# Duo attention and PReLU MLP on one core: the first 400 steps in another order

## Chip, cores, metric

The kernel runs on 1 core of one Trainium2 chip. The metric is the device time of one execution in microseconds (us), lower is better. The core has a matrix engine (PE, with its weight loads shown as PEld), three engines for elementwise work (DVE, ACT, POOL) and SP, which here only issues DMAs. Each takes its own instructions strictly in the order in which the program lists them, and waits at semaphores for the others.

## Reference

Attention for 4 batches of 8 heads, 768 tokens, head size 64, and then a two-layer MLP on the 3072 tokens.

```python
scores = scale * np.matmul(q, k.transpose(0, 1, 3, 2))
# causal mask for heads 0, 2, 6 ("retrieval"); the other heads ("streaming") keep
# of the causal part only the 4 first keys and the last 64
scores = np.where(mask[None], scores, -1e9)
a = np.exp(scores - np.max(scores, axis=-1, keepdims=True))
a = a / (np.sum(a, axis=-1, keepdims=True) + 1e-09)
x = (a @ v).transpose(0, 2, 1, 3).reshape(3072, 512)
h = x @ w_in                                   # 512 -> 2048
g = np.maximum(h, 0.0) + alpha * np.minimum(h, 0.0)
out = g @ w_out                                # 2048 -> 512
```

Inputs and outputs are float32; the kernel computes in bfloat16 with float32 sums.

## The kernel before

The work is cut into some thousand named items. `ORDER`, a string near the top, lists the 1076 names, and the last loop of the kernel calls them one after the other. Each call appends its instructions to the queues of the engines that it uses, so ORDER sets the order on every engine, and with it the order of the DMA issues, of the PSUM banks that are taken and given back (`take`, `give`: the free bank that has been free longest), and of the rings of buffers.

The heads are treated in 16 segments n, each a pair of heads of one batch (`PAIRS`: one batch is four segments). The names:

- `Lq`, `Lk`, `Lv` n: loads of q, k and v by SP (one half of Lk0 by ACT). Segment n uses buffer n % 4 of each, so that a load waits for the casts of segment n-4.
- `Cq`, `Ck`, `Cv`: casts to bfloat16, on POOL, DVE or ACT by the strings CQ, CK, CV. `Tq`, `Tk`: transposes on PE for n < 8; `tq`, `tk`: their copies out of PSUM (DVE for the first four `tk`, ACT for `tq` and for `tk` of n from 4 on). From n = 8 on a DMA transposes.
- `S` n.hh.m: scores of head hh, part m, on PE; `s`: their exp on ACT; `m`: mask on DVE (n from 4 on; for n < 4 the mask is added by a matmul with `nms` or `nmr`). `A`: probabilities times v on PE; `a`: division on DVE; `X`, `x`: transposed into `xT` (PE and DVE for n < 4).
- `P` t.f: first MLP layer for token block t (512 or 256 tokens) and rows f, on PE; P0.f.0 to P0.f.2 are its parts for f < 6. `p`: relu of the negative on ACT; `g`: the PReLU on DVE (L609). `O` t.s.u: a quarter of the second layer; `o`: the copy on ACT and the store.
- `wi0` to `wi7`, `wo0` to `wo3`: loads of the MLP's weights, issued by POOL. They fill what P and O of those rows need.
- `warm`: matmuls of zeros on PE, as fillers (L687; 32, 3, 14 and six times 4 of them). `id`, `idf`, `zero`, `one`, `busy`, `kz`, `vz`, `qz`, `sz`, `so`, `ro`, `vo`, `nz`, `kfz`: constants and memsets. `nr` makes mr_near on POOL from `one`; `ns` makes ms_near with twelve POOL instructions. `La`, `Al`, `al`: the slopes.

Scores of n from 4 on are not issued at once. They are gathered as a burst until an item comes that may not stand beside them:

```python
if min(columns) < SPLIT:            # SPLIT = 576; columns of the two heads hh
    for x in burst:
        nc.tensor.matmul(*x[3:6], start=True, stop=True)      # L423, 128 rows
else:                               # alternately, each on its own 64 rows: L430
```

With enough columns of both heads the two halves of the array work side by side (L430); else every matmul takes the whole array (L423).

Of the kernel before, what the change touches and what calls it, by code (L numbers as in the profile page):

```python
# [19 lines left out]
X0 s2.0.1 x0 wi6 s2.0.2 wi7 Lv3 Lq5 Tq3 tk3.1 S2.0.0 wi5 m4.0.2 warm6 S2.1.0 A1.0 a1.0 Lk4 s2.0.0 A2.0 S2.1.1 A1.1  # L20
a2.0 tq3 s2.1.0 a1.1 S3.0.0 s2.1.1 s3.0.0 A2.1 a2.1 S3.1.1 X1 S3.0.1 s3.0.1 Lk5 wi4 kfz2 Cv3.0 Cq5 Lk7 wi2 X2 Ck4.0
s3.1.1 S3.1.0 x1 P0.0.0 x2 P0.0.1 A3.0 P0.1.0 P0.1.1 Lk6 Lq4 Lq6 Ck4.1 kfz3 nr Cv3.1 s3.1.0 A3.1 Lv7 Lv5 Lq7 Ck5.0 wi3
a3.0 P0.2.0 Tq5 tq5 P0.3.0 P0.3.1 a3.1 X3 x3 ns kfz1 P0.2.1 Tk4 near2 P1.2 P0.1.2 P0.2.2 P0.0.2 p1.2 p0.1 g0.1 Ck5.1
P1.0 P0.3.2 g1.2 P0.15 tk4.0 p0.2 g0.2 p0.15 wo0 p1.0 Lk8 near0 g0.15 g1.0 ro1 P1.12 P1.14 m12.1.2 p0.0 g0.0 wo1 tk4.1
p1.12 P0.14 g1.12 p0.14 g0.14 P0.13 p0.13 g0.13 P0.11 p1.14 Tk5 Ck7.1 g1.14 P1.10 tk5.0 p0.11 p1.10 Ck6.0 Ck7.0 g0.11
m8.0.2 tk5.1 wo2 Lv6 Lv4 P0.10 P0.8 p0.8 Tk7 g1.10 wo3 Cq4 Lk9 P0.12 P1.8 p0.10 g0.8 p0.12 g0.10 Tq4 P0.6 P0.9 p0.3
Ck6.1 g0.3 tq4 P0.4.0 P0.5.0 Tk6 P0.4.1 p1.8 g1.8 tk7.0 p0.9 g0.9 Cq6 P0.5.1 P0.5.2 p0.5 g0.12 p0.6 tk6.1 P0.4.2 g0.6
g0.5 tk6.0 S4.0.5 P0.7 p0.7 P1.6 g0.7 P1.4 s4.0.5 p0.4 Tq6 m4.1.2 tk7.1 g0.4 Cv5 p1.6 g1.6 O0.1.0 tq6 S4.0.3 O0.2.0
O0.2.1 S5.1.1 S5.0.0 S4.0.1 S6.1.0 m14.0.2 p1.4 g1.4 s5.0.0 O0.1.1 s4.0.3 s4.0.1 O0.2.2 S5.0.2 S5.1.0 S4.0.2 S5.1.2
s6.1.0 m4.0.1 Cv7 O0.3.0 s5.0.2 s5.1.2 s5.1.1 s4.0.2 O0.1.2 s5.1.0 O0.1.3 o0.1 Cq7 Cv4 O0.3.1 m5.1.0 m8.1.2 m5.0.2  # L30
m4.0.3 m5.1.2 S4.0.0 S4.1.4 S5.0.1 S4.0.4 S4.1.0 s4.0.4 s5.0.1 Lk10 m5.0.1 O0.2.3 O0.3.2 Tq7 m5.0.0 o0.2 s4.1.0 m4.0.4
m5.1.1 A5.1 s4.0.0 m4.0.0 a5.1 O0.3.3 tq7 S7.0.0 S7.0.1 S4.1.3 S7.1.1 S6.0.5 S4.1.1 m4.0.5 s4.1.4 o0.3 Lq9 s4.1.3 Ck8
m4.1.3 A5.0 a5.0 X5 s4.1.1 A4.0 s7.0.0 s7.1.1 Lk11 Lq8 s7.0.1 a4.0 s6.0.5 near1 m7.0.0 m7.1.1 m4.1.0 O1.1.0 S7.1.0
S6.0.4 S7.0.2 S4.1.5 S6.0.1 S7.1.2 S6.1.1 O1.1.1 Cv6 s7.1.0 O1.0.0 s4.1.5 m7.0.1 s6.1.1 m4.1.5 m6.1.1 s7.1.2 m6.1.0
s7.0.2 m7.0.2 S6.0.2 S4.1.2 S6.1.2 S6.0.0 s6.0.4 s4.1.2 s6.0.1 s6.1.2 O1.0.1 m6.0.5 m7.1.0 m4.1.1 m4.1.4 m7.1.2 m6.1.2
S6.0.3 A4.1 s6.0.0 m6.0.0 m6.0.1 A7.1 O1.1.2 A6.1 s6.0.3 m6.0.4 m6.0.3 s6.0.2 a4.1 a6.1 A6.0 A7.0 a6.0 O1.1.3 O0.0.0
O0.0.1 O0.0.2 O1.0.2 m10.0.2 O1.0.3 O0.0.3 o0.0 X4 X6 a7.1 a7.0 X7 P2.9 P2.3 p2.9 P3.4 Ck9 Cq9 g2.9 P2.14 p2.14 g2.14
Cq8 p3.4 Lq10 Lq11 Dk8.0 P2.10 p2.10 Dk9.1 o1.0 p2.3 g2.3 g3.4 Dk8.1 P3.2 P3.14 P3.12 P2.8 Dq8 P2.1 P3.8 o1.1 p3.2
Dk9.0 Lv10 g2.10 Dq9 p3.14 P2.7 Ck10 g3.2 p3.12 g3.12 g3.14 P2.2 p2.2 g2.2 Cq10 Dq10 P2.11 p2.1 g2.1 p2.11 p2.8 g2.11
P3.6 P2.5 p2.5 g2.5 P2.13 p2.13 g2.8 g2.13 P2.0 p2.0 g2.0 p2.7 P3.0 p3.0 P2.4 S8.0.5 Lv8 Lv11 P2.15 P2.12 s8.0.5 Cq11  # L40
g3.0 p2.15 g2.7 g2.15 S8.0.0 p2.12 g2.12 Ck11 p3.6 S9.0.2 P2.6 p2.6 g3.6 s8.0.0 p2.4 g2.4 g2.6 s9.0.2 p3.8 P3.10 g3.8
p3.10 O3.0.0 O2.0.0 S8.1.5 s8.1.5 O3.0.1 O2.0.1 g3.10 m8.0.0 Cv8 S8.1.3 S9.0.0 S8.0.3 S9.1.1 S8.0.1 S9.1.0 s8.1.3
s9.1.0 s8.0.1 s9.0.0 s8.0.3 m8.0.3 m8.0.1 O2.0.2 O2.0.3 o2.0 Dk10.1 Lv9 m9.0.0 Cv9 m8.0.5 Dk11.0 m9.1.0 m9.0.2 S8.0.4
S9.0.1 S10.1.1 S8.1.4 Dq11 s8.1.4 Lq13 Lk13 O3.0.2 Dk10.0 s9.1.1 s10.1.1 s9.0.1 s8.0.4 O3.0.3 o3.0 Dk11.1 S10.1.0
S10.1.2 m9.0.1 S11.0.2 S9.1.2 S8.0.2 S11.0.0 s9.1.2 Cv10 m9.1.1 A9.0 s11.0.2 s10.1.0 O2.3.0 m9.1.2 A9.1 a9.0 a9.1 X9
s10.1.2 s11.0.0 O2.3.1 Lq15 Lv14 Lq12 S8.1.0 S11.0.1 S10.0.3 m10.1.0 s8.0.2 S10.0.1 S8.1.2 S8.1.1 S10.0.0 O2.3.2
s8.1.2 s8.1.0 m8.1.4 Cq13 s11.0.1 s8.1.1 m11.0.2 m10.1.2 m8.0.4 m11.0.0 A8.0 s10.0.0 m8.1.5 m10.1.1 O2.3.3 a8.0
S11.1.2 S10.0.4 S11.1.0 S10.0.5 S10.0.2 m8.1.3 m11.0.1 s10.0.3 s10.0.1 S11.1.1 s11.1.2 A10.1 s11.1.1 O2.2.0 O2.1.0
s10.0.4 m6.0.2 m10.0.1 Cv11 m8.1.1 m8.1.0 a10.1 m10.0.4 Ck13 m10.0.0 m11.1.2 A11.0 A8.1 O2.1.1 s10.0.2 s10.0.5 o2.3
s11.1.0 Dk13.0 m11.1.1 m10.0.3 m10.0.5 m11.1.0 A10.0 a11.0 a8.1 a10.0 O3.1.0 A11.1 Cq12 O2.2.1 O2.2.2 O2.2.3 a11.1 X8  # L50
O2.1.2 O3.1.1 O3.1.2 X10 o2.2 O3.1.3 O2.1.3 X11 P4.11 o2.1 P4.14 P5.14 p5.14 P4.4 P4.6 Lk12 P5.0 g5.14 Ck12 p4.4 p4.6
p4.11 P4.13 g4.6 p4.14 g4.11 Lq14 g4.14 P5.12 P4.5 P4.12 p4.13 Dq12 o3.1 p5.0 g4.13 Cq14 g5.0 Dk13.1 p4.5 g4.5 g4.4
Cv14 P4.9 p4.9 g4.9 P4.2 P5.2 Dq13 p5.12 g5.12 P4.10 p5.2 P4.8 P4.1 p4.12 g4.12 g5.2 p4.10 g4.10 Lv15 Dk12.0 Dk12.1
Lv12 p4.1 Lk14 Lv13 Lk15 g4.1 P4.7 P4.0 p4.2 g4.2 p4.8 g4.8 p4.0 p4.7 g4.7 P4.15 Cv12 S13.0.1 s13.0.1 S12.0.5 S12.0.3
P4.3 P5.4 g4.0 s12.0.3 p4.3 s12.0.5 S12.1.5 S12.0.1 S12.0.0 S13.1.1 s13.1.1 Dq14 g4.3 Cq15 Ck14 m12.0.3 O4.3.0 s12.1.5
s12.0.1 O4.3.1 O4.3.2 s12.0.0 p4.15 g4.15 P5.6 P5.10 S12.1.1 S12.0.4 S12.0.2 p5.4 S13.1.0 g5.4 p5.6 s12.0.4 Dk14.0
P5.8 s13.1.0 s12.0.2 p5.8 s12.1.1 m12.0.0 g5.6 O4.3.3 Ck15 p5.10 g5.8 m12.0.1 g5.10 m12.0.4 O5.1.0 Cv13 O5.1.1 O5.1.2
o4.3 Dk14.1 S14.1.1 S14.0.0 S12.1.4 S14.0.1 S14.1.0 S13.0.2 m12.1.1 s14.1.0 s13.0.2 O4.2.0 m12.0.5 A12.0 s14.0.1
s12.1.4 O5.1.3 Dk15.1 s14.1.1 Dk15.0 s14.0.0 a12.0 m14.0.1 Dq15 o5.1 O4.2.1 S13.1.2 S12.1.2 S14.1.2 S14.0.4 m13.1.0
m14.0.0 m13.0.1 S14.0.5 S13.0.0 O4.2.2 O4.2.3 s13.1.2 m13.1.2 m13.1.1 s13.0.0 s14.0.4 s14.0.5 m13.0.2 S12.1.0 m12.1.5  # L60
s14.1.2 S12.1.3 S15.0.0 S14.0.3 m13.0.0 A13.1 o4.2 s12.1.0 s12.1.2 A13.0 s15.0.0 O5.0.0 s12.1.3 s14.0.3 m14.0.4 Cv15
a13.1 O5.0.1 a13.0 S15.0.1 S15.0.2 m12.1.0 S15.1.0 S15.1.2 S15.1.1 S14.0.2 O4.1.0 s15.0.2 s15.1.0 m12.1.4 s14.0.2
s15.1.1 m14.1.1 m14.0.5 m14.1.2 m12.1.3 m14.1.0 A12.1 m14.0.3 A14.1 A14.0 a14.0 s15.1.2 a14.1 m15.0.2 s15.0.1 a12.1
O4.1.1 X13 O4.0.0 O4.0.1 O4.0.2 O4.0.3 m15.0.0 m15.1.1 O4.1.2 m15.0.1 m15.1.2 m15.1.0 A15.0 o4.0 A15.1 a15.0 O4.1.3
a15.1 O5.0.2 X15 O5.0.3 X14 x15 o4.1 o5.0 X12 P6.11 p6.11 P6.2 P6.15 P6.10 p6.10 P7.4 P6.0 P6.1 g6.11 g6.10 p6.1 P6.6
P7.8 p6.15 g6.15 g6.1 p6.0 g6.0 P6.5 p7.4 p6.5 p6.6 g7.4 g6.6 g6.5 P6.3 P6.12 P7.2 p6.3 p6.12 g6.12 p6.2 g6.2 P6.4
p7.8 P7.6 P6.14 g6.3 g7.8 p7.6 p6.4 g7.6 g6.4 P7.10 P6.7 P6.8 p6.8 p6.7 P7.0 P6.9 P6.13 g6.7 p7.2 g7.2 g6.8 p7.10
g7.10 p6.9 P7.14 O6.3.0 P7.12 p6.13 g6.13 p7.12 O6.0.0 O6.0.1 O6.1.0 p7.0 g7.0 g6.9 O6.3.1 O7.0.0 O6.3.2 O6.1.1 p7.14
p6.14 g6.14 g7.12 O6.3.3 o6.3 O6.0.2 O6.1.2 O6.1.3 o6.1 O6.0.3 o6.0 O6.2.0 O6.2.1 O6.2.2 O7.0.1 O7.0.2 O6.2.3 o6.2
# [777 lines left out]
```

## Time and profile before

| | us |
|---|---|
| median of 3 runs | 229.61 (229.19 to 230.07) |
| profiled execution | 229.83 |
| its span, first to last instruction | 228.0 |
| PE busy | 222.4 |
| DVE / ACT / POOL busy | 151.6 / 139.6 / 45.8 |
| granted TensorE clock | 1.0 |

The span is what the views show; some 1.8 us of the execution lie around it. A matmul's end is modelled, and matmuls overlap, so a busy PE may still be waiting a little. In a timeline a row is a start, a length, the engine, line and operation, the tiles, how many were merged, and in brackets the idle time before and what ended it. In a row of stretches the first number is the length, then follow the busy times of PE, PEld, DVE, ACT and POOL with counts, the granted clock, the busy share of the DMA engines and GB/s.

### The profile page before, as it was taken

The numbers are of one execution on the slowest core, as the hardware profiler recorded it, in microseconds if no ns is written. First come the engines' busy times: TensorE is split into PE (matmuls) and PEld (weight loads), VectorE is DVE, ScalarE is ACT, GpSimd is POOL, SyncE is SP. The second block draws the span as 40 slices with busy tenths as digits, with TensorE's granted clock in tenths as the row PEclk, the third lists the DMA queues.
The fourth block names the chain that finished last, engine by engine and source line by source line (L and its number), as shares of the span: only waits on it lengthen the run. The fifth ranks groups of instructions, "written<-read, shape, count | busy, mean of one in ns | idle before, by whom it ended". The sixth has DMA issues, their size and how long they took to land.

```text
span 228.0 us, 5239 instructions
## 1 busy us (share of the span) xinstructions
PE 222.4 (98%) x2005; PEld 135.9 (60%) x2005; DVE 151.6 (66%) x395; ACT 139.6 (61%) x284; POOL 45.8 (20%) x91
## 2 busy tenths in 40 slices
...
DMA  6999999999998798989969899995821420000213
GB/s 190 313 229 210 286 223 262 206 197 241 206 287 142 132 204 227 172 192 181 254 153 199 194 266 146 218 166 107 132 93 38 116 95 0 0 4 0 88 66 123
DMA packets 95417, 37.39 MB, mean 164 GB/s; under 512 B 82440, under 2 KB 93600, under 8 KB 95392
## 3 DMA queue, kind: packets, MB, share of 16 engines
...
q10 hardware_dynamic: 464, 0.40, 0.5%
q8 instruction: 15, 0.25, 0.5%
...
## 4 chain that ended last, share of the span: by engine, by line
PE 92%; ACT 3%; DVE 2%; issue 1%; DVEq 0%; ACTq 0%
PE P L597 35%; PE P L617 34%; PE P L552 7%; PE P L430 4%; PE P L687 3%; PE P L413 2%; PE P L363 2%; PE P L636 2%; ACT neg L602 1%; PE P L501 1%; DVE kT L392 1%; PE P L423 1%; PE P L577 1%; ACT kT L392 1%; ACT eS L523 1%
## 5 line engine op out<-in xcount | busy, mean ns | idle before, releaser
L609 DVE SCALAR_TENSOR_TENSOR g<-neg,oma,P 128x256 bf16<-128x256 f32 (+1 forms) x128 | 71.0, 608 | 35.9 <-ACT neg L602 35.5
L597 PE MATMUL P<-xT,w_in_b 128*128 128x512 bf16 (+1 forms) x512 | 86.5, 326 | 0.0
L617 PE MATMUL P<-w_out_b,g 128*128 128x512 bf16 x368 | 85.4, 379 | 0.0
L602 ACT ACTIVATE neg<-P 128x512 f32<-128x512 f32 x96 | 54.4, 600 | 27.2 <-PE P L597 22.6
L597 PEld LDWEIGHTS <-w_in_b 128*128 128x128 bf16 x512 | 49.5, 98 | 31.7 <-DVE g L609 0.2
L617 PEld LDWEIGHTS <-g 128*128 128x128 bf16 x368 | 33.8, 98 | 37.2 <-issue 1.2
L469 ACT ACTIVATE eR<-P 128x448 bf16<-128x448 f32 (+4 forms) x63 | 37.1, 636 | 5.4 <-PE P L430 2.3
L623 ACT COPY ot<-P 128x512 f32<-128x512 f32 x23 | 13.8, 602 | 37.8 <-PE P L617 32.9
L627 POOL DMA_DIRECT2D out_dram<-ot x18 | 10.3, 571 | 113.2 <-ACT ot L623 113.0
L517 ACT ACTIVATE eS<-P 128x352 bf16<-128x352 f32 x45 | 21.0, 493 | 3.7 <-PE P L430 3.7
L563 DVE TENSOR_TENSOR xn<-P,rcp 128x448 bf16<-128x448 f32 (+1 forms) x32 | 19.5, 608 | 1.1
L528 DVE TENSOR_TENSOR eS<-eS,ms_near 128x352 bf16<-128x352 bf16 x45 | 14.3, 334 | 4.4 <-ACT eS L517 4.2
L479 DVE TENSOR_TENSOR eR<-eR,mr_near 128x128 bf16<-128x128 bf16 (+5 forms) x54 | 12.1, 252 | 4.0 <-ACT eR L469 4.0
L430 PE MATMUL P<-qT,kT 64*128 64x176 bf16 (+13 forms) x181 | 11.7, 251 | 0.3 <-DVE g L609 0.3
L430 PEld LDWEIGHTS <-kT 64*128 64x128 bf16 x181 | 7.2, 94 | 7.6 <-issue 6.8
L413 PE MATMUL P<-qT,kT 128*128 128x192 bf16 (+14 forms) x68 | 11.3, 251 | 0.3 <-ACT eS L523 0.3
L552 PE MATMUL P<-vb,eS 128*128 128x65 bf16 x260 | 11.0, 193 | 0.4 <-DVE eS L528 0.4
L552 PEld LDWEIGHTS <-eS 128*128 128x128 bf16 x260 | 9.7, 97 | 2.9 <-DVE eS L528 0.6
L562 DVE RECIPROCAL rcp<-P 128x7 f32<-128x7 f32 (+1 forms) x32 | 6.3, 198 | 7.1 <-PE P L552 6.9
L552 PE MATMUL P<-vb,eR 128*128 128x65 bf16 x276 | 10.1, 192 | 0.0
L552 PEld LDWEIGHTS <-eR 128*128 128x128 bf16 x276 | 9.4, 97 | 1.2
L645 DVE COPY ot<-P 128x128 f32<-128x128 f32 x1 | 0.3, 292 | 14.3 <-PE P L636 14.3
...
## 6 DMA issues: line engine op xcount, KB each, us to landing
...
```

Source lines behind the costliest of these rows:

```text
L413: nc.tensor.matmul(to, keys, queries, start=True, stop=stop)
L430: nc.tensor.matmul(to, keys[own], queries[own], start=True, stop=True)
L469: nc.scalar.activation(ebuf[n, hh][:, lo:hi].rearrange("p (x c) -> p x c", x=len(parts)), P[:, got[0]:got[0] + len(parts), 0:(hi - lo) // ...
L517: nc.scalar.activation(slots, sc[:, 0:352].rearrange("p (s c) -> p s c", c=176), AF.Exp, scale=scale)
L528: nc.vector.tensor_tensor(slots, slots, ms_near[:, 0:2, :] if m == 0 else ms_near[:, 1:3, :], op=ALU.mult)
L552: nc.tensor.matmul(pav[:, i, :], e[:, o:o + 128], vv[:, j, hh, 0:D + 1], start=(m == 0), stop=(m == len(terms) - 1))
L563: nc.vector.tensor_tensor(xn[n][:, 0:nt, D * hh:D * hh + D], pav[:, :, 0:D], rcp.to_broadcast([128, nt, D]), op=ALU.mult)
L597: nc.tensor.matmul(psg[:, w * i:w * (i + 1)], w_in_b[:, c, 128 * fb:128 * (fb + 1)], xT[:, c, o:o + w], start=(x == 0), stop=(x == 3))
L602: nc.scalar.activation(neg[t, f], bank(held["P", t, f][0]), AF.Relu, scale=-1.0)
L609: nc.vector.scalar_tensor_tensor(g_buf[t % 2][:, fb, 0:w], neg[t, f][:, c], oma[:, fb:fb + 1], bank(got[0])[:, c], op0=ALU.mult, op1=ALU.add)
L617: nc.tensor.matmul(bank(held["O", t, s][0]), g_buf[t % 2][:, f, 128 * s:128 * (s + 1)], w_out_b[:, f, :], start=(f == 0), stop=(f == 15))
L623: nc.scalar.copy(ot, bank(got[0]))
```

## The change

The first 400 of the 1076 names in ORDER stand in another order; the rest of the list, and the rest of the kernel, are untouched. The loads Lq, Lk and Lv keep their sequence among each other. The two lists hold the same names. Around the changed part the old and the new list begin and end like this (lines of the list, cut):

```diff
-busy zero La id warm0 kz3 Lq0.0 sz1 vz2 nms nmr so1 vz0 Lq0.1 Lk1 warm8 warm5 warm3 kz1 qz0 one Lq1 Lk0 Ck0.0 Cq0.0
-Tq0.0 tq0.0 Tk0.0 qz kz0 kz2 idf warm2 Lk2 tk0.0 Ck1.0 Ck1.1 Cq0.1 Tk1 S0.0.1 s0.0.1 Tq0.1 S0.0.0 Cq1 warm7 Lv0 tk1.0
-sz2 vz1 vz3 Tq1 Lq2 Ck0.1 S0.0.2 s0.0.0 tk1.1 Tk0.1 Ck2.1 tq1 S1.1.0 s0.0.2 Ck2.0 warm4 tq0.1 nz0 s1.1.0 Cq2 tk0.1 Cv0
...
+vz2 id busy warm4 warm0 warm5 vz0 qz0 Lq0.0 sz2 so2 Lq0.1 zero vz3 nms Lk1 Lq1 sz1 Cq0.1 nmr Ck1.1 kz1 La Lk0 Ck1.0
+kz0 Cq1 Cq0.0 Tq0.0 Ck0.0 Tk0.0 tk0.0 Lk2 Ck2.0 Lv0 warm2 tq0.0 S0.0.0 s0.0.0 qz S0.0.1 Tk1 warm3 warm6 vo kz2 Ck0.1
+vz1 Ck2.1 Tq1 s0.0.1 tq1 Tq0.1 tk1.1 S0.0.2 s0.0.2 Cv0 tk1.0 m4.0.2 warm7 tq0.1 Lq2 S1.1.0 Tk0.1 tk0.1 S1.0.0 ro0
...
```

The item O1.1.0 is the last PE work before the two lists agree; the score bursts on both sides of it are the same in both programs, though gathered from other places of the list. On the engines the change does this, as the built programs show:

- PE: 40 filler matmuls stand ahead of the first transpose, Tq0.0, where there were 44. S0.0.0 comes before S0.0.1, Tk0.1 after S1.1.0, A0.0 before S0.1.1. Seven small pieces of scores (S5.1.1, S5.0.0, S5.0.2, S5.1.0, S4.0.1, S4.0.3, S5.0.1) stand between groups P of the MLP's first layer, where one, S4.0.5, stood. 168 matmuls are on line 430 and 36 on line 423; there were 181 and 23, and the columns on line 423 are 7080 after 4424.
- ACT: the exps of those pieces stand among the relus; the copies tk6, tk7 and tq6 stand behind them.
- DVE: vz2 ahead of busy, kz1 and kz0 ahead of Cq0.0; `one` behind the first g (g1.0), where it stood ahead of Cq0.0; the masks m5.0.0 and m5.1.0 among the g.
- POOL: kz3 behind Cq2; Cv0 ahead of Cq2; kfz3 ahead of wi6; Ck4.0 ahead of wi2; wo0 to wo3 ahead of ns and, like it, behind nr, which waits for `one`.
- SP: the same instructions in the same sequence.

More of the change, by code (lines that the diff above doesn't have):

```diff
@@ L20 @@
[L20 to L69, printed above, removed]
```

56 lines of the change are left out of this document (53 added, 3 removed).

## The prediction

> **What bounds the kernel now.** I read the page first, its busy times and slices, then PE's busy time in stretches of 5.7 us, then PE's timeline, and last the timelines of the engines that feed PE.
>
> ```profile
> span 228.0 us, 5239 instructions
> PE 222.4 (98%) x2005; PEld 135.9 (60%) x2005; DVE 151.6 (66%) x395; ACT 139.6 (61%) x284; POOL 45.8 (20%) x91
> DMA  6999999999998798989969899995821420000213
> L617 PE MATMUL P<-w_out_b,g 128*128 128x512 bf16 x368 | 85.4, 379 | 0.0
> L597 PE MATMUL P<-xT,w_in_b 128*128 128x512 bf16 (+1 forms) x512 | 86.5, 326 | 0.0
> ```
>
> PE is the bound: 222.4 of 228.0 us, and neither of its two big groups has idle time ahead of it. The DMA engines are full for the first two thirds, so the loads come as fast as they can whatever stands around them. A new order of the same work can only change PE's waits, how the score matmuls are paired, and where fillers (L687) run.
>
> ```profile
> 5.70:11.40 5.70, 5.23 (x76) 4.51 (x74) 4.29 (x14) 3.87 (x6) 4.54 (x8) 1.00 1.13 313
> 11.40:17.10 5.70, 5.54 (x95) 4.76 (x93) 3.98 (x13) 4.94 (x8) 3.58 (x7) 1.00 0.99 229
> 22.80:28.50 5.70, 5.51 (x94) 4.68 (x91) 4.91 (x11) 2.98 (x5) 5.24 (x12) 1.00 1.15 286
> 51.30:57.00 5.70, 5.39 (x33) 2.13 (x30) 3.78 (x7) 5.44 (x13) 0.63 (x1) 1.00 1.13 241
> 62.70:68.40 5.70, 5.25 (x78) 3.23 (x76) 4.81 (x15) 5.16 (x13) 2.06 (x3) 1.00 1.11 287
> ```
>
> The first number after the comma is PE's busy time: these five stretches lack 0.47, 0.16, 0.19, 0.31 and 0.45 us. The timeline shows where (start, length, idle before):
>
> ```profile
> 1.07 4.88 PE L687 MATMUL P<-busy 128*128 128x128 bf16 x44 [1.07 <-DVE zero L288]
> 6.78 0.95 PE L687 MATMUL P<-busy 128*128 128x128 bf16 x14
> 10.92 0.49 PE L363 MATMUL P<-ident,g 128*128 128x128 bf16 x6 [0.47 <-DVE kT L394]
> 12.97 0.24 PE L413 MATMUL P<-qT,kT 128*128 128x192 bf16 x1 [0.16 <-ACT eS L523]
> 25.95 0.24 PE L413 MATMUL P<-qT,kT 128*128 128x192 bf16 x1 [0.19 <-ACT eS L523]
> 51.30 1.03 PE L617 MATMUL P<-w_out_b,g 128*128 128x512 bf16 x4
> 52.35 0.35 PE L423 MATMUL P<-qT,kT 128*128 128x64 bf16 x2
> 54.98 0.36 PE L430 MATMUL P<-qT,kT 64*128 64x320 bf16 x4 [0.29 <-DVE g L609]
> 57.59 3.63 PE L617 MATMUL P<-w_out_b,g 128*128 128x512 bf16 x16
> 61.15 0.70 PE L430 MATMUL P<-qT,kT 64*128 64x448 bf16 x8
> 64.59 0.45 PE L552 MATMUL P<-vb,eS 128*128 128x65 bf16 x9 [0.45 <-DVE eS L528]
> 67.52 0.81 PE L617 MATMUL P<-w_out_b,g 128*128 128x512 bf16 x3
> ```
>
> A matmul of 512 columns is shown with 0.379 us, yet sixteen take 3.63: one starts every (3.63-0.38)/15 = 0.217, so a modelled end lies 0.16 behind the next start, and each bracket hides that much. The five waits cost 0.63, 0.33, 0.35, 0.45 and 0.61. Two show no bracket: the four quarter matmuls at 51.30 should take 0.87 and the next starts after 1.05 (0.18), and some 0.15 lies at 41.9. Together 2.7 us: all that a better order could win. From 67.52 (O1.1.0) PE's order is the same in both programs and what PE has done until then is the same, so I ask when O1.1.0 starts.
>
> **The change part by part.** Nothing is added or removed but one thing: the pairing of scores. The items are in the new ORDER; the engines' queues follow from it.
>
> Start. These rows price it (DVE, ACT, POOL):
>
> ```profile
> 1.20 0.17 DVE L288 MEMSET vf<- 128x128 f32 x1
> 3.10 0.06 DVE L288 MEMSET one<- 128x1 bf16 x1
> 3.96 1.75 DVE L288 MEMSET kT<- 128x896 f32 x2
> 5.41 0.51 ACT L328 CAST g<-kf 128x384 bf16<-128x384 f32 x1 [2.40 <-DMA kf<-in_k_dram]
> 18.36 0.95 POOL L348 CAST vb<-vf 128x896 bf16<-128x896 f32 x1
> 19.38 0.63 POOL L306 COPY vb<-vb 4x192 f32<-4x192 f32 x2
> ```
>
> vz2 goes ahead of busy on DVE, so the fillers start some 0.15 later, at 1.2. There are 40 instead of 44 ahead of Tq0.0; a cold one costs 4.88/44 = 0.11, a warm one 0.95/14 = 0.06 (with its end), so moving four behind the clock's rise saves 4 x 0.05 = 0.2. Tq0.0 then begins at 5.6 and Tk0.0 at 6.25, still behind the cast that ends at 5.92. On DVE, Cq0.0 goes behind kz1 and kz0 (1.75): done at about 4.65, under the fillers. Net -0.05.
>
> To 31 us. I chained the new order by hand with these durations. Waits that I find: S1.1.0 for tq1 on ACT (0.25), S2.0.1 for s1.1.1 (0.1), A1.0 for Cv1, which on POOL ends 1.6 (0.95 and 0.63) after Cq3, at 20.0, where PE is there at 19.85 (0.15), P0.0.0 for x1 (0.1), A3.1 for Cv3.1, now behind x2 on DVE (0.1), X3 for a3.1 (0.15). P1.2, at 31.05 before, starts at 30.5. Old waits gone: S0.1.0 and Tk0.1 now stand where tk1.0 and tk0.1 are done.
>
> POOL, and what queues behind one memset.
>
> ```profile
> 28.46 1.27 POOL L659 TENSOR_SCALAR_AFFINE_SELECT mr_near<-one 128x1248 bf16<-128x1248 bf16 x1
> 30.81 0.34 POOL L665 TENSOR_SCALAR_AFFINE_SELECT ms_near<-one 128x176 bf16<-128x176 bf16 x1
> 34.80 3.01 POOL L696 DMA_DIRECT2D w_out_b<-in_moe_w_out_dram  x4
> 40.58 0.83 POOL L315 CAST natq<-qf 128x768 bf16<-128x768 f32 x1 [2.77 <-DMA qf<-in_q_dram]
> 19.03 8.90 SPq L223 DMA_DIRECT2D kf<-in_k_dram  x8
> 27.98 4.32 SPq L209 DMA_DIRECT2D qf<-in_q_dram  x2
> ```
>
> "one" (0.06) moves on DVE from 3.10 to behind g1.0 (P1.0's group is out at 32.2, its relu at 33.0, its g 0.87 later), about 33.9, and nr on POOL waits for it. Behind nr stand kfz1, the four issues of w_out (3.0), ns (3.4, from 30.81 to the next line's start near 34.2) and Cq4. So w_out is issued at 35.4 (0.6 later), and Cq4 ends at 33.9 + 1.27 + 0.2 + 3.0 + 3.4 + 0.83 = 42.6 (41.4 before). Tq4, which needs it, is reached by PE at 44.1: 1.5 to spare, cost nothing; past that PE pays one for one. SP issues without a pause (8.90 for eight, the next at 27.98), its sequence is the same, so loads land when they did; w_in issues move by under 0.7.
>
> 31 to 67 us.
>
> ```profile
> 32.12 1.08 ACT L602 ACTIVATE neg<-P 128x512 f32<-128x512 f32 x2 [1.66 <-PE P L597]
> 39.39 0.71 ACT L392 COPY kT<-P 64x672 bf16<-64x672 bf16 x1
> L602 ACT ACTIVATE neg<-P 128x512 f32<-128x512 f32 x96 | 54.4, 600 | 27.2 <-PE P L597 22.6
> L609 DVE SCALAR_TENSOR_TENSOR g<-neg,oma,P 128x512 bf16<-128x512 f32 x64 | 45.7, 741 | 22.4 <-ACT neg L602 22.1
> 31.05:51.30 20.25, 20.25 (x152) 13.11 (x150) 16.21 (x36) 18.26 (x38) 7.19 (x19) 1.00 1.20 223
> 32.12:66.52 34.40, 33.64 (x249) 18.98 (x248) 25.08 (x57) 31.36 (x68) 9.34 (x20) 1.00 1.15 229
> ```
>
> A group P1 takes PE 4 x 0.217 = 0.87, its relu 0.48 start to start (1.08-0.60), its g 0.74 on DVE. The new order scatters seven small score pieces (S5.1.1, S5.0.0, S5.0.2, S5.1.0, S4.0.1, S4.0.3, S5.0.1) between P1 groups, whose exps ACT does under P1, and puts the copies tk6, tk7, tq6 (0.71 for the longest part of a tk) behind them. Chaining PE, ACT and DVE: O0.1.0 starts at 49.65 (51.30 before), Tk6 at 50.9 behind g0.5, P1.6 at 52.1 behind g0.6 (0.1 lost on both), Tq7 at 60.45 with Cq7 done at 60.1, A5.1 at 60.8 with its masks done at 59.9, O1.1.0 at 65.8. Before, A5.1 waited 0.61 for its masks and a score burst 0.45 for g; both are early now, because ACT (31.36 of 34.40 busy) had its exps sooner. Next late is ACT's tk7.0, at 57.0, where PE is at 56.95.
>
> Pairing. Scores of two heads run side by side when both halves of a burst hold 576 columns. The new lists have 36 unpaired matmuls (L423) against 23, and 7080 of their columns against 4424: 2656 columns run alone at 0.217/512 us each, 1.1 us, where in pairs they'd take half. That is 0.55 more; with two bursts fewer, each with about 0.12 lost at its edges (61.15 to 61.79 is 0.64 for 2144 paired columns, that is 0.45), it is +0.3.
>
> **Sum.** -0.05 at the start, -2.7 old waits, +0.95 new ones (0.25+0.1+0.15+0.1+0.1+0.15+0.1), +0.3 pairing: -1.5 (the chain itself says 67.52-65.8 = 1.7). A hand chain misses hand-overs; I take 0.3 off: -1.2. From 67.5 on PE has no bracket until the end region in this trace and the SP queue has gaps, so I let the whole of it reach the end. The profiled execution took 229.83 (span 228.0 and 1.8 around it): 228.6 on its scale, and on the median of 229.61, 0.2 lower, 228.4.
>
> **A rule against the row.** The row of 44 fillers at 0.11 each, and the next 14 at 0.06, shows the PE clock rising between 5.95 and 6.8, some 5 us after the first filler. The Trainium skill ("TensorE: Matmul & The Clock Gate", Part 1) says that the activity window which opens the clock runs freely, 3.4 us long, and does not start with the kernel; by it a start 0.15 later can as well open the clock one window later, an estimate of up to 1.7 us more (3.4 at half speed), and the sum would be +0.5. The row alone says that the rise stays where it is.
>
> **Rivals.** The waits only move. ACT waited 34.40-31.36 = 3.0 us between 32.12 and 66.52; if it waits as long in the new order, O1.1.0 comes only by the 0.55 won up to P1.2, and the 0.3 of pairing is lost: 229.4. For it: four links have under 0.4 to spare (P1.10, Tk6, P1.6, Tq7). Against: the exps are early where PE waited.
>
> ACT's queue becomes the bound, and the kernel slower. Place: relus, exps and copies in one queue from p1.2 to tk7.0. A relu is 0.60 long and costs 0.48 only when the next is ready; in the new order some 25 of ACT's instructions follow one of another kind and wait for fresh PE output. If each pays the 0.12 that overlap saved, ACT is 3.0 late at tk7.0, and PE, which has 0.3 to spare, pays 2.7 of it: -1.2+2.7 = +1.5, 231.1. It takes the side from ACT 1.5 late at tk7.0 (58.5). For it: ACT is busy 18.26 of 20.25 in that stretch. Against: in the old order the same mix ran without that loss.
>
> The clock rises later. At half speed the 4.1 us from 6.3 to 10.45 would take 4.1 more at most, of which the waits at 10.92 and 12.97 (1.0) swallow a part; half of the rest is 1.5: 229.9 to 231.5. Or it rises sooner, and the fillers end sooner for nothing.
>
> It does nothing to the time: the load queue bounds the whole. Against: PE is 98% busy and POOL's waits for loads lie under it.
>
> **How the numbers follow.** A change under 0.5% (1.15 us) cannot be told from none here: the three runs lie 0.9 apart. Forecast, 60%: 228.4, own range 227.4 (no new waits, no allowance: -2.3) to 229.3 (new waits doubled); two thirds of it, 0.40, lies below 228.46, the rest, 0.20, is the same. Waits move or nothing happens, 15%: the same. ACT, 20%: slower. Clock, 5%: slower 0.04, same 0.01. So faster 0.40, same 0.36, slower 0.24. The range 227.4 to 231.2 leaves out the upper half of ACT's case and of the clock's and a little below.
>
> **What would show it.** Right: O1.1.0 (first L617 after the A4.0 run) near 66; no bracket at A5.1 and in the 54 to 55 us burst; P1.2 near 30.5; nr on POOL waiting for DVE until about 34; L423 x36. Wrong: ACT shown as releaser of PE between 44 and 60; Tq4 waiting for POOL natq; the second half not shorter by the same amount; or the filler row longer than 4.6 us.

## The result, and the profile after

The changed kernel takes 228.14 us (median of 20 runs, 226.87 to 229.77), the kernel before took 229.49 beside it (228.93 to 230.34): 0.9951 [0.9935, 0.9967] of the time. That is 1.35 us less by the medians and 1.1 by the ratio, which is not the ratio of the medians. Runs more than 1.5% above the fastest of their kernel are left out of every median, ratio and span below (none here; one each in E1 and E6, three each in E3 and E12). The forecast was 228.4, within 227.4 to 231.2, and faster. The profiled execution of the changed kernel, 229.76 with a span of 228.1, is one of the upper end of its 20 runs; by itself it shows no gain at all, and why is the main thing to be learned here.

The page of the changed kernel (header, busy times, and two of its groups):

```profile
span 228.1 us, 5213 instructions
PE 220.6 (97%) x1977; PEld 136.9 (60%) x2005; DVE 151.5 (66%) x395; ACT 139.3 (61%) x284; POOL 46.2 (20%) x91
L413 PE MATMUL P<-qT,kT 128*128 128x192 bf16 (+14 forms) x68 | 11.2, 251 | 0.2 <-DVE kT L386 0.2
L552 PE MATMUL P<-vb,eS 128*128 128x65 bf16 x260 | 10.8, 193 | 1.6 <-DVE vb L343 1.4
```

28 of PE's 2005 matmuls have no record here, so 220.6 can't be set against the 222.4 of before. The wait in the last row is new: PE stood 1.6 us in front of the products with v, 1.4 of them for DVE's cast of v (0.4 before, for DVE's masks). The stretches that the prediction showed, with the one from 28.50 added (length, then busy times of PE, PEld, DVE, ACT and POOL):

```profile
5.70:11.40 5.70, 5.70 (x82) 5.27 (x83) 4.17 (x11) 3.94 (x5) 3.58 (x8) 1.00 1.12 312
11.40:17.10 5.70, 5.53 (x99) 4.86 (x97) 5.43 (x15) 5.00 (x8) 4.66 (x8) 1.00 1.02 248
22.80:28.50 5.70, 5.23 (x79) 4.30 (x77) 4.41 (x9) 2.84 (x5) 4.25 (x9) 1.00 1.15 277
28.50:34.20 5.70, 4.51 (x53) 3.66 (x54) 3.30 (x7) 2.58 (x4) 2.19 (x4) 1.00 1.20 224
51.30:57.00 5.70, 5.65 (x47) 3.64 (x46) 3.50 (x11) 5.37 (x14) 0.81 (x1) 1.00 1.12 244
62.70:68.40 5.70, 5.59 (x77) 3.35 (x76) 2.74 (x10) 4.79 (x12) 2.63 (x4) 1.00 1.05 262
```

Three of the five old holes are closed or nearly so: PE lacks nothing in the first stretch, 0.05 and 0.11 in the last two (0.47, 0.31 and 0.45 before). The second stretch still lacks 0.17 (0.16 before). A new hole begins in the row from 22.80 and takes 1.19 of the next. PE's timeline around it (start, length, idle before), and then what DVE and POOL did:

```profile
26.45 0.56 PE L552 MATMUL P<-vb,eS 128*128 128x65 bf16 x13
26.84 1.24 PE L597 MATMUL P<-xT,w_in_b 128*128 128x512 bf16 x5
29.46 0.22 PE L552 MATMUL P<-vb,eS 128*128 128x65 bf16 x2 [1.38 <-DVE vb L343]
29.86 0.49 PE L552 MATMUL P<-vb,eS 128*128 128x65 bf16 x11 [0.18 <-DVE vb L306]
30.18 1.03 PE L597 MATMUL P<-xT,w_in_b 128*128 128x512 bf16 x4
```

```profile
26.22 0.56 DVE L582 COPY xT<-P 128x768 bf16<-128x768 bf16 x1 [0.20 <-PE P L577]
26.79 2.62 DVE L343 CAST vb<-vf 128x448 bf16<-128x448 f32 x1
29.44 0.36 DVE L306 COPY vb<-vb 4x192 f32<-4x192 f32 x1
...
26.39 0.62 POOL L692 DMA_DIRECT2D w_in_b<-in_moe_w_in_dram  x1
27.00 0.52 POOL L328 CAST natm<-kf 128x384 bf16<-128x384 f32 x1
27.45 0.84 POOL L315 CAST natq<-qf 128x768 bf16<-128x768 f32 x1
28.22 0.91 POOL L288 MEMSET natk<- 128x960 f32 x1
29.05 0.61 POOL L692 DMA_DIRECT2D w_in_b<-in_moe_w_in_dram  x1
```

Cv3.1, a cast of 448 columns on DVE, took 2.62 us; the same row is 0.86 in the kernel before. It came up 0.21 before POOL's issue of wi2 ended (27.01). Then POOL ran Ck4.1, Cq5 and nz1 without a gap, until 29.12, and the cast ended at 29.41, 0.28 later. In the kernel before the same cast came up under POOL's Cq5, which ended at 26.86, and ended 0.28 after it, at 27.14 (DVE, then POOL):

```profile
26.28 0.86 DVE L343 CAST vb<-vf 128x448 bf16<-128x448 f32 x1
26.04 0.82 POOL L315 CAST natq<-qf 128x768 bf16<-128x768 f32 x1 [0.40 <-DMA qf<-in_q_dram]
26.81 0.61 POOL L692 DMA_DIRECT2D w_in_b<-in_moe_w_in_dram  x1
```

A3.1 on PE needs that cast, and everything behind it on PE was 1.9 us late. The rest of the trace is what was forecast, as the three stretches behind P1.2 show (P1.2 to O0.1.0, O0.1.0 to O1.1.0, O1.1.0 to the end), of the kernel after:

```profile
32.35:51.55 19.20, 19.09 (x134) 12.32 (x136) 15.34 (x32) 17.49 (x37) 9.18 (x21) 1.00 1.21 226
51.55:67.55 16.00, 15.89 (x156) 9.29 (x155) 8.60 (x32) 14.79 (x34) 3.57 (x5) 1.00 1.08 237
67.55:228.10 160.55, 156.31 (x1263) 89.33 (x1281) 102.01 (x267) 87.78 (x189) 10.20 (x17) 1.00 0.66 133
```

and the last two of the kernel before:

```profile
51.30:67.52 16.22, 15.46 (x144) 7.75 (x142) 9.88 (x27) 14.10 (x33) 3.56 (x5) 1.00 1.09 240
67.52:228.00 160.48, 157.57 (x1285) 89.38 (x1281) 101.67 (x268) 87.86 (x189) 10.11 (x17) 1.00 0.66 134
```

Behind P1.2 the new order won 20.25-19.20 = 1.05 and 16.22-16.00 = 0.22, together 1.27; ahead of it, in this execution, it lost 32.35-31.05 = 1.30. Only the sum of the two stretches behind P1.2 compares the same work: ahead of O0.1.0 the old list also has Tk6, Tk7, Tq6, S4.0.5 and P1.6, and the new one the seven score pieces.

### The profile page after: what moved, and what is told of

It is laid out like the page before. It is cut to its first block, busy times and chain, and to the rows that moved or that the text cites. A ratio compares the mean times of both kernels' runs of the same rounds, so it can differ in the third digit from the quotient of the medians.

```text
span 228.1 us, 5213 instructions
## 1 busy us (share of the span) xinstructions
PE 220.6 (97%) x1977; PEld 136.9 (60%) x2005; DVE 151.5 (66%) x395; ACT 139.3 (61%) x284; POOL 46.2 (20%) x91
## 4 chain that ended last, share of the span: by engine, by line
PE 96%; DVE 2%; issue 1%; DVEq 0%
PE P L597 36%; PE P L617 35%; PE P L552 7%; PE P L430 4%; PE P L413 3%; PE P L687 3%; PE P L363 2%; PE P L636 2%; PE P L423 1%; DVE vb L343 1%; PE P L501 1%; PE P L577 1%; PE P L361 1%; PE P L462 0%; DVE xT L582 0%
## 5 line engine op out<-in xcount | busy, mean ns | idle before, releaser
L609 DVE SCALAR_TENSOR_TENSOR g<-neg,oma,P 128x256 bf16<-128x256 f32 (+1 forms) x128 | 70.9, 608 | 36.5 <-ACT neg L602 36.0
L597 PE MATMUL P<-xT,w_in_b 128*128 128x256 bf16 (+1 forms) x501 | 85.7, 325 | 0.6
L617 PE MATMUL P<-w_out_b,g 128*128 128x512 bf16 x351 | 83.1, 379 | 1.0 <-issue 0.2
L617 PEld LDWEIGHTS <-g 128*128 128x128 bf16 x368 | 33.9, 98 | 37.3 <-issue 1.0
L479 DVE TENSOR_TENSOR eR<-eR,mr_near 128x128 bf16<-128x128 bf16 (+5 forms) x54 | 10.8, 229 | 4.7 <-ACT eR L469 4.5
L413 PE MATMUL P<-qT,kT 128*128 128x192 bf16 (+14 forms) x68 | 11.2, 251 | 0.2 <-DVE kT L386 0.2
L430 PE MATMUL P<-qT,kT 64*128 64x176 bf16 (+10 forms) x168 | 10.5, 251 | 0.0
L430 PEld LDWEIGHTS <-kT 64*128 64x128 bf16 x168 | 6.7, 94 | 6.2 <-issue 5.5
```

Source lines behind the costliest of these rows:

```text
L413: nc.tensor.matmul(to, keys, queries, start=True, stop=stop)
L430: nc.tensor.matmul(to, keys[own], queries[own], start=True, stop=True)
L597: nc.tensor.matmul(psg[:, w * i:w * (i + 1)], w_in_b[:, c, 128 * fb:128 * (fb + 1)], xT[:, c, o:o + w], start=(x == 0), stop=(x == 3))
L609: nc.vector.scalar_tensor_tensor(g_buf[t % 2][:, fb, 0:w], neg[t, f][:, c], oma[:, fb:fb + 1], bank(got[0])[:, c], op0=ALU.mult, op1=ALU.add)
L617: nc.tensor.matmul(bank(held["O", t, s][0]), g_buf[t % 2][:, f, 128 * s:128 * (s + 1)], w_out_b[:, f, :], start=(f == 0), stop=(f == 15))
```

## Experiments

Theory 1: DVE's cast is held as long as POOL works without a break, in some executions only, and these make the upper end of the runs. Theory 2: the loads land at other times and the clock rises at another moment in each execution, and that makes the width. The first four ran together (kernel before: 229.55), the next four (229.37), and the last four (229.16). One table of all profiled executions, read from the timelines (us): the start of S0.0.0, the length of DVE's cast of Cv3.1, and the four stretches into which S0.0.0, P1.2, O0.1.0 and O1.1.0 cut the rest. In the old list S0.0.1 stands ahead of S0.0.0 (it starts at 7.91 in before and at 8.06 in E4), so the first number and the stretch to P1.2 of these two rows can't be set against those of the others.

| | S0.0.0 | cast | to P1.2 | to O0.1.0 | to O1.1.0 | to the end |
|---|---|---|---|---|---|---|
| before | 8.68 | 0.86 | 22.4 | 20.25 | 16.2 | 160.5 |
| after | 7.53 | 2.62 | 24.8 | 19.2 | 16.0 | 160.5 |
| E1 cast on ACT | 7.17 | ACT | 22.9 | 19.2 | 16.0 | 160.5 |
| E2 wi2 later | 7.61 | 0.39 | 23.4 | 19.3 | 16.0 | 160.5 |
| E3 new, then old | 7.55 | 0.39 | 22.9 | 20.5 | 15.6 | 160.5 |
| E4 old, then new | 8.83 | 0.42 | 22.3 | 19.5 | 16.0 | 160.5 |
| E5 new again | 7.21 | 0.39 | 22.9 | 19.2 | 16.0 | 160.5 |
| E6 memsets early | 6.89 | 0.53 | 23.7 | 19.2 | 16.0 | 160.9 |
| E7 ACT, one early | 7.08 | ACT | 22.9 | 19.2 | 16.0 | 161.2 |
| E8 ACT, then old | 6.98 | ACT | 22.9 | 22.4 | 15.5 | 160.5 |
| E9 more memsets | 7.50 | 0.82 | 23.0 | 19.2 | 16.0 | 160.5 |
| E10 the same, ACT | 7.05 | ACT | 22.9 | 19.2 | 16.0 | 160.5 |
| E11 no pairs | 6.97 | 0.39 | 22.9 | 19.2 | 16.7 | 163.9 |
| E12 short start | 6.99 | ACT | 23.5 | 19.2 | 16.4 | 160.5 |

### E1: Cv3.1 on ACT

```diff
-cast_of("PV"[hh])(vv[:, :, hh, 0:D], vf[n % NF][:, :, hh, :])
-sinks(..., [hh], (nc.gpsimd.tensor_copy, nc.vector.tensor_copy)[hh])
+cast_of("PA"[hh])(vv[:, :, hh, 0:D], vf[n % NF][:, :, hh, :])
+sinks(..., [hh], (nc.gpsimd.tensor_copy, nc.scalar.copy)[hh])
```

> The new order, with Cv3.1 (the cast of one head of v, and its small copy) on ACT in place of DVE. Theory 1: in the new order DVE's cast stands against an unbroken run of POOL instructions (Ck4.1, Cq5, nz1) and gets through only when that run breaks; in the profiled run it took 2.62 us where 0.86 was seen before, and PE stood 1.4 us at A3.1. Whether it meets the run differs from execution to execution, so the times of the new kernel lie between 226.9 and 229.8. Then ACT, idle from 26.4 to 31.6, casts in 0.6 us, A3.1 has no wait, the times lie within 0.8 us of each other, at about 227.2 (2.2 under before). Theory 2: the width comes from when loads land or when the clock rises; then median about 228.1 and the same width. By the prediction's chain: P1.2 at 30.5, O1.1.0 at 65.8.

227.91 us, 0.9924 [0.9897, 0.9951]. The wait at A3.1 is gone and the stretch to P1.2 is 22.9. The span, 225.8, is 2.3 under that of after: 1.9 from this stretch and 0.36 from the start. By time the forecast missed: I had 227.2 within 0.8 us, and the eight runs spread over 1.6 us (227.28 to 228.86) with a median that can't be told from the new order's own in E5 (228.03).

### E2: wi2 issued behind nz1

```diff
-... near2 Ck4.0 P0.0.0 wi2 s3.0.1 ... X3 nz1 tk4.1 ...
+... near2 Ck4.0 P0.0.0 s3.0.1 ... X3 nz1 wi2 tk4.1 ...
```

> The new order, with wi2 (a DMA issue on POOL that parts Ck4.0 from Ck4.1) moved behind nz1, so that POOL runs Ck4.0, Ck4.1, Cq5, nz1 without a break for 2.7 us, from about 25.9. Theory 1: the cast on DVE, due at 26.8, is held in every execution until POOL's run ends at about 28.7: every run near 229.3, narrow. Theory 2: the place of wi2 does not touch PE: median about 228.1, width as with the new order.

228.03 us, 0.9931 [0.9906, 0.9957]; theory 1's 229.3 in every run did not come. In its profile POOL's run hadn't begun when the cast came up: the load for Ck4.0 landed only at 27.86 (25.94 in after), the cast took 0.39, and Tk4 waited some 0.45 (a bracket of 0.28, and the 0.16 that each bracket hides) for Ck4.1, whose load landed at 29.13. Removing one issue is no handle on the hold as long as a load decides when POOL's run starts.

### E3 and E4: the halves

```diff
 E3: the new list up to P1.2, then the names that are left, in the old order
 E4: the old list up to P1.2, then the names that are left, in the new order
```

> The new order up to the first P1.2, then the remaining items in the old order. By the prediction the first part alone brings 0.55, and the second part's gain (1.1 with the pairing) is gone: 229.0 where DVE's cast gets through. Theory 1: the cast is in the first part, so the times go from 228.9 to 231 as the runs of the new order did over 2.9 us. Theory 2 (width from later loads): narrow, about 229.0. 23 unpaired matmuls as before.

> The old order up to the first P1.2, then the remaining items in the new order. By the prediction's chain the stretch from P1.2 to O1.1.0 takes 35.3 us where it took 36.5: about 228.3. Theory 1: the cast meets POOL as in the old kernel, so the times are as narrow as before (1.4 us). Theory 2: as wide as the new order's.

E3: 229.22 us, 0.9986 [0.9955, 1.0017]. E4: 228.67 us, 0.9977 [0.9951, 1.0003]. By time, each half alone is within what can't be told from no change. By the table, P1.2 to O1.1.0 takes 36.1 with the old list behind P1.2 and 35.5 with the new one (36.5 before, 35.2 after), and E3 comes to P1.2 at 30.46, 0.6 ahead of the kernel before: by one trace each, the gain is made of both parts. E4's 228.67 lies above the 228.3 that I had. E3's times spread over 2.9 us, as theory 1 had it, but E4's over 2.0 where it had 1.4. E3 also shows what doesn't hold the cast. The timelines of POOL and DVE:

```profile
26.62 0.66 POOL L692 DMA_DIRECT2D w_in_b<-in_moe_w_in_dram  x1
27.54 0.50 POOL L328 CAST natm<-kf 128x384 bf16<-128x384 f32 x1 [0.26 <-DMA kf<-in_k_dram]
...
26.80 0.39 DVE L343 CAST vb<-vf 128x448 bf16<-128x448 f32 x1
```

The cast ran its 0.39 us wholly beside the issue of wi2. In after it came 0.21 before that issue ended, with POOL's next cast right behind: too late by some 0.2, as I read it.

### E5: the new order once more

> The new order once more, unchanged, beside the next three. Theory 1 (a cast of Cv3.1 that is caught under an unbroken run of POOL makes the upper runs): its runs fall again into a lower group near 227.3 and an upper one near 229.3, and its profiled execution belongs to the upper group just when that cast takes over 1.5 us in it (P1.2 at 32.4 or so; about 30.5 and a cast of 0.4 in the lower one). Theory 2 (the landing times of the loads and the moment of the clock's rise make the width): the same width, but a profiled execution with a short cast may be as late as 229. Median 228.1 by both.

228.03 us, 0.9956 [0.9932, 0.9981]. Its profiled execution has a span of 225.9, 2.2 less than that of after, for the same program. PE's timeline at the same place, then DVE's and POOL's:

```profile
26.52 1.24 PE L597 MATMUL P<-xT,w_in_b 128*128 128x512 bf16 x5
27.60 0.56 PE L552 MATMUL P<-vb,eS 128*128 128x65 bf16 x13
```

```profile
26.47 0.39 DVE L343 CAST vb<-vf 128x448 bf16<-128x448 f32 x1
...
24.47 0.34 POOL L306 COPY vb<-vb 4x192 f32<-4x192 f32 x1
26.70 0.50 POOL L328 CAST natm<-kf 128x384 bf16<-128x384 f32 x1 [1.89 <-DMA kf<-in_k_dram]
```

Ck4.0 had to wait for its load until 26.70, so POOL stood still when the cast came up. The cast took 0.39, its last 0.16 beside Ck4.0, which kept its 0.50, and PE has no gap. Of the 2.2 us between two executions of one program, 1.9 are this (24.8 against 22.9) and 0.3 are the start. Set beside the runs (by their spans, since what lies around a span differs by itself, from 1.66 to 2.80 us in these 32 runs): of the 32 spans of the new order, here and in the first measurement, 23 lie at 225.2 to 226.5 and 9 at 227.2 to 228.1, with none between. With the cast on ACT (E1, E7, E10: 27 spans) 26 lie at 225.5 to 227.1, and the last at 227.2, the lower edge of the upper group. So the upper group goes with the cast on DVE; that each of the nine runs had the hold is inferred, since only one of them was traced.

### E6: POOL made busy earlier

```diff
-... Cv3.0 s3.0.0 ... Ck4.0 P0.0.0 wi2 ... Cq5 m14.0.2 a3.1 X3 nz1 ...  (nz0 behind P0.9)
+... Cv3.0 nz1 nz0 s3.0.0 ... Ck4.0 P0.0.0 ... Cq5 wi2 m14.0.2 a3.1 X3 ...
```

> The new order, with the memsets nz1 and nz0 put right behind Cv3.0 on POOL (ahead of Ck4.0) and the load wi2 issued behind Cq5: POOL is busy without a pause from the end of Cv3.0 near 24.6 to the end of Cq5 near 28.5, whenever the load for Ck4.0 lands. Theory 1: DVE's cast of Cv3.1, due at about 26.8, is held in every execution until that run ends or pauses; it takes 1.3 us or more, P1.2 comes at 31.7 or later, the lower group is gone, and the median is near 229.2. Theory 2: the cast is short or its length does not matter; the median is 228.1 as for the new order.

228.08 us, 0.9938 [0.9914, 0.9962]. The cast took 0.53, not 1.3: the memsets ended at 26.40, Ck4.0 had to wait for its load until 27.27, and the cast ended at 26.68, 0.28 after the memsets, in that gap. The 0.8 that the stretch to P1.2 is longer came in at another place: Ck4.1's load landed at 28.66, and Tk4 waited. Not the run that I meant to make, so nothing follows for theory 1.

### E9 and E10: POOL busy for certain

```diff
-... Cv3.0 s3.0.0 ... Ck4.0 P0.0.0 wi2 ... Cq5 ...
+... Cv3.0 nz1 nz1 nz1 s3.0.0 ... Ck4.0 P0.0.0 ... Cq5 wi2 ...     (E10: and the edit of E1)
```

> The new order with three more memsets of nz1's buffer (0.9 us each, the same zeros) on POOL right behind Cv3.0, and wi2 issued behind Cq5: POOL is busy from 24.8 to 27.5 for certain, and then casts as the loads of Ck4.0 and Ck4.1 have landed. Theory 1: DVE's cast of Cv3.1, due at about 26.5, is held until POOL first pauses; it takes 1.2 to 2.9 us in the profiled execution, P1.2 comes at 31.3 or later, and the spans lie 1 to 2 us above those of the next kernel; the lower group near 226 is gone. Theory 2 (only landing times and the clock's rise): the cast takes 0.4 to 0.6 and the spans are those of the next kernel.

> The same kernel with Cv3.1 on ACT: POOL is busy for just as long, but no cast of DVE stands under it. Theory 1: P1.2 at 30.1 to 30.5, median near 228.0, no span above 227.2 or one of them at most. If the memsets cost time in another way (Ck4.1 late, Tk4 waiting for it on PE), this kernel shows it as well, and only the difference of the two counts for the cast.

E9: 228.02 us, 0.9941 [0.9917, 0.9966]; E10: 227.53 us, 0.9922 [0.9887, 0.9957]. The timelines of DVE and POOL in E9, and of POOL in E10:

```profile
26.77 0.82 DVE L343 CAST vb<-vf 128x448 bf16<-128x448 f32 x1
...
24.51 2.80 POOL L288 MEMSET natk<- 128x960 f32 x3
27.26 1.10 POOL L328 CAST natm<-kf 128x384 bf16<-128x384 f32 x2
```

```profile
24.35 2.80 POOL L288 MEMSET natk<- 128x960 f32 x3
27.09 0.96 POOL L328 CAST natm<-kf 128x384 bf16<-128x384 f32 x2
```

Theory 1 in my wording fails here. The cast was held, but only to the end of the memsets (27.31) and not until POOL paused: it ended at 27.58, 0.28 later, and POOL's two casts took 1.10 where they take 0.96 beside a cast on ACT. The 0.28 comes back in every profile where the cast took more than 0.39: before, after, E4, E6 and E9 show its end 0.28 to 0.29 us behind the end of a memset or cast of POOL. So I read these rows as a lock: the cast of DVE can't run while POOL runs a memset or a cast, and E9's cast of POOL had to wait for it in turn; at a seam of POOL, from one instruction to the next, either may come next. In after two such seams (27.45, 28.22) passed by the waiting cast, here the first one let it in. Which of them does is not settled. PE lost 0.1 by it (A3.1 starts 1.68 behind P0.0.0's first record in both), and E9's spans, 225.6 to 226.7, have no upper group.

### E7: the memset one back at the start, with the cast on ACT

```diff
-... Lq1 sz1 Cq0.1 ... P0.13 Lq4 one p0.1 ...     (and the edit of E1)
+... Lq1 sz1 one Cq0.1 ... P0.13 Lq4 p0.1 ...
```

> The new order with Cv3.1 on ACT, as before, and the one-column memset called one back at the start on DVE (behind sz1), so that nr on POOL no longer waits for the first g, and the loads of w_out are issued 3 to 5 us earlier. By the prediction's step the memset's place costs nothing: the same as with the cast on ACT alone, 227.9, within 0.4; P1.2 to O0.1.0 stays at 19.1. The rival: w_out that moves earlier takes the loads of k and q for segments 5 to 7 some 2 us of queue, and Tk6 or Tk7 waits on PE: 0.5 to 1 us slower.

228.15 us, 0.9951 [0.9931, 0.9972], against 0.9924 [0.9897, 0.9951] for E1: not to be told apart, and the stretches up to O1.1.0 are the same to 0.05. But nr starts at 33.54 here as well, since Ck5.1, ahead of it on POOL, waits for its load until 33.08: w_out was issued only 0.2 earlier (34.89 against 35.11), and the rival wasn't put to the test.

### E8: the new order up to O0.1.0, then the old one

```diff
 the new list up to g0.6, the item ahead of O0.1.0, then the names that are left, in the old order; with the edits of E7
```

> The new order up to the item ahead of O0.1.0, with Cv3.1 on ACT and the memset one at the start, and from there the names that are left in the old order. The stretch from O0.1.0 to O1.1.0 took 15.64 us where the old list followed (with the old middle part ahead) and 16.0 where the new one did. If the old tail is better by its own order, O1.1.0 comes 0.4 us earlier and the median is near 227.5. If the 15.64 came from what the old middle part had already done, nothing is won: 228.0, and a wait for masks or for the exps on ACT shows ahead of A5.1.

231.1 us, 1.0081 [1.0053, 1.0109]: slower, and both of my forecasts missed. The old list has Tk7, Tk6, S4.0.5, P1.6 and Tq6 ahead of O0.1.0, so the middle stretch is longer; but the two stretches to O1.1.0 together are 37.9 against 35.2. What follows is the ACT rival of the prediction, made by accident. The timeline of PE, and ACT's ahead of it:

```profile
52.30 2.76 PE L617 MATMUL P<-w_out_b,g 128*128 128x512 bf16 x11 [0.35 <-DVE g L609]
56.43 0.31 PE L423 MATMUL P<-qT,kT 128*128 128x176 bf16 x2 [1.36 <-ACT qT L368]
```

```profile
50.97 0.72 ACT L392 COPY kT<-P 64x672 bf16<-64x672 bf16 x1
...
54.13 0.71 ACT L392 COPY kT<-P 64x672 bf16<-64x672 bf16 x1
55.58 0.79 ACT L368 COPY qT<-P 128x768 bf16<-128x768 bf16 x1
```

The copies tk6 and tk7 stand on ACT one behind the other from 50.97 to 55.06, with one exp between them; tq6 behind them ends at 56.37, and PE waits 1.36 us for it. A third bracket, 0.24 at 51.45, is for DVE's g like the 0.35. With the 0.16 that each bracket hides, the three waits are 2.4 of the 2.7 lost, and ACT's is 1.5 of that. That is what a wait for ACT in this stretch looks like; the new order, which spreads these copies between relus, shows no such bracket.

### E11: no pairs

```diff
-    SPLIT = 576
+    SPLIT = 1 << 20
```

> The new order with the bound SPLIT set so high that no scores are paired. It measures the price in the prediction's pairing term. Between O0.1.0 and O1.1.0 two bursts with 2688 and 2440 columns lose their pairing: half of 5128 columns at 0.217/512 us each is 1.09, less 0.24 for the edges of two paired bursts: the stretch goes from 16.0 to 16.9 by the prediction's price. Paired twice as dear would be 18, at nothing 16.0. Later bursts lose theirs as well, so the whole becomes some 6 to 10 us slower; no forecast is made of that.

231.66 us, 1.011 [1.0057, 1.0163]. The stretch from O0.1.0 to O1.1.0 is 16.66 instead of 16.00, where my price gave 16.9. A burst on PE's timeline in E11, and the same one in after:

```profile
56.50 1.31 PE L423 MATMUL P<-qT,kT 128*128 128x128 bf16 x12
```

```profile
59.02 0.75 PE L430 MATMUL P<-qT,kT 64*128 64x128 bf16 x12
```

Half of 5128 columns is 1.09, and 0.66 were lost: the edges of the two bursts eat 0.43, 0.21 each, where I had 0.12.

### E12: a shorter start

```diff
-... Cq0.0 Tq0.0 ... qz ... vo kz2 ... vz1 ... (warm2, warm3, warm6, warm7, warm8 among the first 110 names)
+... Cq0.0 qz vo kz2 vz1 Tq0.0 ...              (these five fillers behind l0, at the end; and the edit of E1)
```

> A version meant to beat both: the new order with Cv3.1 on ACT, the 34 fillers that stand behind the first transposes put behind the last store, and the memsets qz, vo, kz2 and vz1 put on DVE right behind Cq0.0, where DVE is idle from 4.8 to 6.5. PE loses 1.6 us of fillers until Tq2; of that DVE's chain of copies (tk0.0 to tk0.1, 13.2 at its end) gives back 0.5. P1.2 at 29.6, O1.1.0 at 64.7, median 227.5. Rival: the loads bound that part (Ck4.1 waits for its load until 28, Ck5.1 until 33), PE waits at Tk4 and Tk5 for what it has won, and the median stays at 228.0.

228.84 us, 0.9978 [0.9941, 1.0015]: nothing won. In its profile PE waits 0.55 for tq0.0 where the fillers stood, S0.0.0 still starts at 6.99, the stretch to P1.2 is 23.5, with a bracket of 0.21 at Tk4 for Ck4.1 (the rival of the expectation) among others, and A4.0 waits 0.24 for Cv4. Its spans reach from 225.5 to 228.8; why they are wider than those of E1 its one trace doesn't show.

No version beats the changed kernel for certain: the lowest, E10 and E1, have intervals that overlap with it.

## Why the prediction was right

**Direction, size and place.** I gave 1.2 us, 1.35 came by the medians (1.1 by the ratio). E5 is the execution that the chain described:

| | forecast | E5 | after |
|---|---|---|---|
| P1.2 | 30.5 | 30.13 | 32.35 |
| O0.1.0 | 49.65 | 49.35 | 51.55 |
| A5.1 | 60.8 | 60.45 | 62.64 |
| O1.1.0 | 65.8 | 65.36 | 67.55 |

Each is 0.3 to 0.45 early in E5. O1.1.0 to the end was 160.5 in every profile with pairs but E6 and E7 (160.9, 161.2), so a gain ahead of it reaches the end, as I had let it.

**Start, -0.05: right.** First filler at 1.21 (I said 1.2), Tq0.0 at 5.58 (5.6), 40 fillers in 4.45. The clock's rise moves what follows by up to 0.7 (S0.0.0 at 6.89 to 7.61 in the table), so a term of this size can't be seen in the total.

**Old waits, -2.7: right but for one.** The stretches of after show them gone. S0.1.0 still waits for tk0.1, 0.21 in E5 and 0.33 in after (0.17 in a bracket, the 0.2 of the page's L413 row, and the hidden 0.16); I had taken that for done.

**New waits, +0.95: the step that failed, for one term.** Of the seven that I named none is over 0.1 in E5. The one that counted, A3.1 for Cv3.1, was on my list at 0.1, by where the cast stands in DVE's queue; nothing in my chain asked what POOL does while DVE casts. It cost 1.9 in the traced execution. The chain also let the loads land when they did, for which it had no row: Ck4.0's load, which starts POOL's run beside that cast, landed at 25.94 in after and at 26.70 in E5. With spans: the 23 lower runs have a median of 225.9, 1.7 under the 227.6 of the kernel before beside E5, which is the chain's 1.7; the nine upper ones have 227.6, no gain. 23/32 x 1.7 = 1.2, near the 1.35 measured. So the 0.3 that I took off for missed hand-overs fits the median for another reason than I gave, and that is luck: most executions have no loss, and by their spans a quarter have a large one.

**The rule that bears on it.** E9 shows one engine held by the other, both ways, 0.43 us and 0.14. The Trainium skill ("SBUF — State Buffer", section "🔬 SBUF: two separate sides") says that DVE, in a mode that takes two ports, and GpSimd share a pair of ports as an exclusive lock: whichever starts first has it for the whole instruction, and the other fully blocks. That this cast is in such a mode no run here shows. E9 agrees with the exclusion. After does not show who starts first as the one that decides: there the cast's row begins at 26.79, ahead of Ck4.1's at 27.00, and the cast still waits, and it loses at two more seams: 2.62 us. Whether the row begins before the cast asks for the ports, or the issue of wi2 held them at its end, no run here settles.

**Pairing, +0.3: too dear by a slip.** The burst that I cited gives 0.64-0.45 = 0.19 at the edges, not the 0.12 that I wrote. E11 has 0.21; two bursts fewer give back 0.42 of the 0.55: +0.13. The lower end of my range has a slip of the same size: without new waits and allowance the sum is -2.45, 227.2, and not -2.3 and 227.4.

**Memset one, no cost: right.** In E1 nr waits for it until 33.76 (33.9 forecast), Cq4 ends at 42.43 (42.6), and Tq4 starts at 43.72 (44.1) without a wait. In after all of it is 2 us later, on PE as well:

```profile
36.00 1.26 POOL L659 TENSOR_SCALAR_AFFINE_SELECT mr_near<-one 128x1248 bf16<-128x1248 bf16 x1 [3.62 <-DVE one L288]
43.88 0.82 POOL L315 CAST natq<-qf 128x768 bf16<-128x768 f32 x1
45.96 0.50 PE L363 MATMUL P<-ident,natq 128*128 128x128 bf16 x6
```

POOL's bracket of 3.62 is harmless: 1.26 us are left between Cq4's end (44.70) and Tq4.

**The middle, 31 to 67: right.** 19.15 and 16.15 forecast for its two stretches, 19.2 and 16.0 measured.

**Rivals.** PE has no bracket at all from 31 to 68 us in after, so ACT releases it nowhere; E8 shows what it costs when it does (1.5). "Waits only move" is what the trace of after alone would make one believe (1.30 lost, 1.27 won); E5 and the spans say that it holds for about a quarter of the runs. "The load queue bounds it" is true of places (Ck4.0, Ck4.1 and Ck5.1 wait for loads), not of the whole. The clock is in the last section.
